# Smaller side steps behind gate tiles, and the last loads in another queue: an S4 convolution woven into a feed-forward network

## The chip, the core and the metric

The kernel runs on one core of a Trainium2 chip. The core has five engines with instruction streams of their own: PE (TensorE, matmuls), DVE (VectorE), ACT (ScalarE), POOL (GpSimd) and SP (SyncE, which here only issues DMAs). Each engine works its instructions off in order and waits on semaphores for what others produce. DMAs are issued by SP, ACT or POOL and carried by 16 DMA engines. The metric is the device time of one execution in microseconds (us). The kernel before takes 1129.19 us, the median of three runs (1126.59 to 1129.72).

## The reference

The input u has 2048 tokens of 576 features. Cut to what matters, the reference computes

```
xn  = layernorm(u)                                  # 2048 x 576
K   = Re( C * exp(dt*A*l) * dt*B  summed over 128 states ), l = 0..2047   # per feature
y   = irfft( rfft(pad(xn)) * rfft(pad(K)) )[:2048] + xn * Dskip            # long convolution
h   = silu(xn @ w1)                                 # w1: 576 x 4608
out = u + y + h @ w2                                # w2: 4608 x 576
```

All in 32-bit floats. The kernel gets that precision on PE by splitting an operand into a high and a low part and adding three products (high*high, high*low, low*high).

## The kernel before

**The main line: the feed-forward network.** Tokens come in four blocks of 512 and the 4608 hidden features in nine chunks of four tiles. A generator `ffn` runs over 36 blocks (half of the tokens, chunk, block in the half). For each it traces four `up` products (L291 to L293: `ph` <- split x times split `w1`, 14 matmuls of 512 columns, in one of two PSUM banks `ps1`) and four `down` products (L316: for each of two column halves, 12 matmuls `po`, in one of three banks `ps2`). ACT takes `ph` through Silu to `gf` (L299) and rounds it to `gh` (L300); DVE forms the low part `gl` (L301). DVE adds `po` to the accumulator `acc` (L320), which frees the bank. Weights are loaded by SP (`w1r` L247 to L249, one buffer; `w2r` L269, two buffers) and split by ACT (`w1h` L260, `w2h` L278) and DVE (`w1l` L262, `w2l` L280).

**The side line: the convolution.** A generator `side` yields at fractions of the main line's 288 steps, and `weave` advances it when the main line has come that far. Its stages, in order:

- `phase0`: token tiles 0 to 7 are loaded, normalised and transposed on PE for the first half.
- The *tables* (`natural`): from dt, A, B, C tables of the kernel K. Among their steps are four Tanh on ACT into `ex` (L447), a reciprocal root into `r` (L451, with a load of ACT's function table ahead of it, and one of Silu's behind), its Square (L452), DVE's products of `ex` and `r` (L457 to L459), and a store `dexp` by SP. In between, the *late tiles* 8, 10, 12 and 14 (two token tiles each) are loaded by SP into the single buffer `xj` (L164), normalised (statistics L180, DVE's half L189, ACT's half L194), transposed by DVE into `tr` (L226) and stored by eight DMAs of SP to `dxt` (L230) and one to `dxn`.
- `kgen` and `spread`: the kernel K and the tokens go through the first stage of a transform (`z` L646, `pu` L153 and L154); the results go to memory as `d1k` (staged by L659, then Dskip added by an accumulating DMA of POOL, L662) and `d1u` (L156).
- `spectral`: for each of 32 frequencies SP loads `ur` and `kr` from there (L746), ACT and DVE split them (`kh` L740, `kl` L741), PE transforms them (`pk`, `pu`, L754), DVE multiplies, PE transforms back (`pb`), and POOL stores the result `yo` to `d` (L705).
- `tail`: the last convolution step. For each of 16 token tiles `j` two DMAs load `ys` from `d` (`conv_load`, L761; eight buffers, six tiles ahead), eight matmuls give `py` (L774, two records each), and DVE adds it to the tile (L780). For tiles 0 to 7 the tile itself, with the feed-forward result, was put aside and is read back as `r0` (L716, four buffers), and POOL stores the output (L171).

**What sets the order.** The traced order is not the final one. A scheduler lays out each engine's instructions from its estimates of durations and from the dependences; `tc.high_priority()` favours some. `behind(ins)` pins what is traced in it to be issued after one named instruction, kept in the dictionary `pins` (the newest `gh`, `gl`, `sd` or weight load). Buffers add waits: a tile in a pool with n buffers waits until its nth predecessor is released. `gate_of(i)` gives the fraction at which the last `up` of block i is traced, so that a step placed there comes just behind that block's gate tiles `gf`, `gh`, `gl`.

Of the kernel before, what the change touches and what calls it, by code (L numbers as in the profile page):

```python
# [2 lines left out]

# [14 lines left out]
P = 128  # L18
# [4 lines left out]
NJ = 16  # L23
# [18 lines left out]
def kernel(  # L42
# [21 lines left out]
    nc = tc.nc  # L64
    FT = 4
# [68 lines left out]
    def behind(ins):  # L134
        return tc.issue_after(ins) if ins is not None else nullcontext()
# [24 lines left out]
    def load_x(j, pool, tag, engines):  # L160

        t = pool.tile([P, 2, D], F32, tag=tag, name=f"{tag}{j}")
        for ps, v, eng in quarters(xv, engines):
            eng.dma_start(t[ps], v[:, j:j + 2])  # L164
        pairs[j] = t
        return t[:, 0, :], t[:, 1, :]
# [30 lines left out]

    def phase0(p0, js):
        j0 = js[0]
        if j0 < 8:  # L200
            xs = load_x(j0, accp, "acc", (nc.sync, nc.scalar) if j0 < 4 else (nc.sync,))
            acc.update(zip(js, xs))
        else:
            xs = load_x(j0, p0, "xj", (nc.sync,))
        if j0:
            normed(p0, js, xs)
        else:
            for j, xj in zip(js, xs):
                normed(p0, (j,), (xj,))
# [23 lines left out]
    def ffn():  # L233
# [6 lines left out]
        def load_w1(half, c, t):  # L240

            f = c * FT + t
            first = half == 0 and c == 0
            r1 = (pa if first and t else wp).tile([P, 5, 2 * P], F32, tag="w1r", name="w1r", bufs=1)
            fs = slice(f * P, (f + 2) * P)
            eng = nc.gpsimd if first and t == 0 else nc.sync
            eng.dma_start(r1[:, 0:4, :], w1[0:512, fs].rearrange("(k p) f -> p k f", p=P))  # L247
            eng.dma_start(r1[0:64, 4, :], w1[512:576, fs])
            pins["load"] = eng.dma_start(r1[64:128, 4, :], w1[512:576, fs]).ins  # L249
            R1[half, c, t] = r1  # L250

        def split_w1(half, c, t):
# [12 lines left out]
        def load_w2(half, c, t):  # L265

            first = half == 0 and c == 0
            r2 = (pa if first and t > 1 else wp).tile([P, D], F32, tag="w2r", name="w2r", bufs=2)
            pins["load"] = nc.sync.dma_start(r2, w2v[:, c * FT + t, :]).ins  # L269
            R2[half, c, t] = r2  # L270

        def split_w2(half, c, t):
# [123 lines left out]
    def natural(nat):  # L396
# [5 lines left out]
        def tl(name):  # L402
            return nat.tile([NP, NT, NS], F32, tag=name, name=name)
# [49 lines left out]
        for i in range(0, 4 * D, D):  # L453
# [4 lines left out]
            v.scalar_tensor_tensor(r[:, c], e, 2.0, r[:, c], op0=ALU.add, op1=ALU.mult)  # L458
            v.scalar_tensor_tensor(ex[:, c], ex[:, c], 1.0, r[:, c], op0=ALU.add, op1=ALU.mult)  # L459
        nc.sync.dma_start(dexp, ex[:, :3 * D].rearrange("n (d k) -> n d k", k=3))  # L460
        pr, pi, t0, t1 = tl("pr"), tl("pi"), tl("t0"), tl("t1")
        v.tensor_mul(pr, cr, br)
        v.tensor_mul(t0, ci, bi)
# [199 lines left out]
                            dskip.unsqueeze(0).broadcast_to([32, D]), accum_op=ALU.add)  # L663

    def spectral():
        def front(k):
            if k % 2 == 0:
                mm = kl.tile([P, 2, 4, P], F32R, tag="mm", name="mm")
                nc.gpsimd.dma_start(mm, cm23[:, k:k + 2])
                mats.append(mm)  # L670
            mk = mats[-1][:, k % 2]
            us, ks = load_split(d1u[k * P:(k + 1) * P, :], "u"), load_split(d1k[k * P:(k + 1) * P, :], "k")
            ka = kl.tile([P, D], F32, tag="ka", name="ka")
            kb = kl.tile([P, D], F32, tag="kb", name="kb", bufs=1)
            y = kl.tile([P, D], F32, tag="y", name="y", bufs=1)
            y2 = kl.tile([P, D], F32, tag="y2", name="y2", bufs=1)
            for h in range(2):
                hs = slice(h * HD, (h + 1) * HD)
                pk = pss.tile([P, 512], F32, tag="pss", name="pk")
                mm3(pk[:, :HD], [(mk[:, 0], mk[:, 1], ks)], hs)  # L680
                nc.scalar.copy(ka[:64, hs], pk[:64, :HD])
                nc.scalar.copy(ka[64:, hs], pk[:64, :HD])
                nc.scalar.mul(kb[:64, hs], pk[64:, :HD], -1.0)
                nc.scalar.copy(kb[64:, hs], pk[64:, :HD])
                pu = pss.tile([P, 512], F32, tag="pss", name="pu2")
                mm3(pu[:, :HD], [(mk[:, 0], mk[:, 1], us)], hs)
                nc.vector.tensor_mul(y[:, hs], pu[:, :HD], ka[:, hs])
                nc.vector.tensor_mul(y2[:64, hs], pu[64:, :HD], kb[:64, hs])
                nc.vector.tensor_mul(y2[64:, hs], pu[:64, :HD], kb[64:, hs])
            nc.vector.tensor_add(y, y, y2)  # L690
            return mk, split_of(y, "y")

        mats = []
        nxt = front(0)
        for k in range(32):
            mk, ys = nxt
            if k < 31:
                nxt = front(k + 1)
            yo = kl.tile([P, D], F32, tag="yo", name="yo")
            for h in range(2):  # L700
                hs = slice(h * HD, (h + 1) * HD)
                pb = pss.tile([P, 512], F32, tag="pss", name="pb")
                mm3(pb[:, :HD], [(mk[:, 2], mk[:, 3], ys)], hs)
                nc.scalar.copy(yo[:, hs], pb[:, :HD])
            nc.gpsimd.dma_start(d2.rearrange("(p k) d -> k p d", k=32)[k], yo)  # L705
            yield 1 + (k + 1) / 32
# [3 lines left out]
    def tail():  # L710

        r0s = {}

        def load_r0(j):
            r0s[j] = yp.tile([P, 2, D], F32, tag="r0", name="r0", bufs=4)
            nc.sync.dma_start(r0s[j], dr0[j * P:(j + 2) * P, :].rearrange("(i p) d -> p i d", p=P))  # L716

        def last(j):
            conv_load(j + AHEAD, 8)
            add_conv(j, r0s[j - j % 2][:, j % 2, :])  # L720
            if j % 2:
                store(r0s[j - 1], j - 1, (nc.gpsimd,))

        steps, at = [], tail_at[0]
        for j in range(8):
            for f in (conv_load, load_r0)[:2 - j % 2]:
                steps.append((at, f, j))
                at += tail_at[1]
        steps += [(tail_at[2] + j * tail_at[3], last, j) for j in range(8)]
        for at, f, j in sorted(steps, key=lambda v: v[0]):  # L730
            yield at
            with behind(pins["load"]):
                f(j)

    yss = {}

    def split_of(t, tag):
        h = kl.tile([P, D], F32R, tag=tag + "h", name=tag + "h")
        l = kl.tile([P, D], F32R, tag=tag + "l", name=tag + "l")
        nc.scalar.copy(h, t)  # L740
        nc.vector.tensor_sub(l, t, h)  # L741
        return h, l

    def load_split(rows, tag):
        t = kl.tile([P, D], F32, tag=tag + "r", name=tag + "r")
        nc.sync.dma_start(t, rows)  # L746
        return split_of(t, tag)

    def mm3(dst, terms, hs):

# [6 lines left out]
    def conv_load(j, first=0):  # L757
        if first <= j < NJ:
            yss[j] = yp.tile([P, 4, HD], F32, tag="ys", name="ys", bufs=AHEAD + 2)
            for h in range(2):  # L760
                nc.sync.dma_start(yss[j][64 * h:64 * h + 64],  # L761
                                  d2[j * 256:(j + 1) * 256, h * HD:(h + 1) * HD].rearrange("(q r) d -> r q d", q=4))

    def add_conv(j, dst):
# [20 lines left out]

    def side():
        nonlocal s4, kl, yp, pa, tail_at
        marks = (0.13, 0.595, 0.822)
        tail_at = (0.895, 0.0045, 0.922, 0.005)
        with tc.tile_pool(name="pa", bufs=4) as pa:  # L790
            for js in ((0, 1), (2, 3), (4, 5), (6, 7)):
# [6 lines left out]
        with tc.tile_pool(name="kf", bufs=1) as kfp:  # L798
            for n in ("f", "phi"):
                kf[n] = kfp.tile([P, D], F32, name=n + "T")  # L800
            with tc.tile_pool(name="nat", bufs=1) as nat, tc.tile_pool(name="pb", bufs=1) as pb:
                nt = natural(nat)
                tiles = iter(range(8, NJ, 2))
                for at, tables in ((0.0, 1), (0.02, 0), (0.035, 0), (gate_of(1), 1), (0.06, 0), (gate_of(2), 1), (0.08, 0), (0.085, 1)):
                    yield at
                    if tables:
                        next(nt, None)
                    else:
                        j = next(tiles)
                        with behind(pins["gl"]):  # L810
                            phase0(pb, (j, j + 1))
            with behind(pins["sd"]):
                nc.gpsimd.dma_start(f1, cf1)
            nc.sync.dma_start(vt, cv)
            with tc.tile_pool(name="up", bufs=1) as up:
                sp = spread(up)
                for n, at in enumerate(kgen()):
                    if n > 1:
                        next(sp, None)
                    yield marks[0] + at * (marks[1] - marks[0])  # L820
                for _ in sp:
                    pass
# [98 lines left out]
```

## Time and profile before

| what | value |
|---|---|
| median of three runs | 1129.19 us (1126.59 to 1129.72) |
| the profiled execution | 1131.96 us, span 1130.2 us, granted clock 0.996 |
| PE busy | 1106.7 us, 98% of the span |
| DVE, ACT, POOL busy | 917.1, 708.7, 78.5 us |
| DMA | 148.56 MB, mean 131 GB/s |

The profile is of one execution. Its span is the time between the first and the last recorded instruction; 1.8 us of the execution's time lie outside it. A row of a group or of the timeline names a line, an engine, an operation and "out<-in" by tile names; the number before it is its duration. Square brackets give the idle time of the engine just before and what ended it ("3.67 <-DVE acc L320": 3.67 us, ended by DVE's instruction of line 320). In the table by windows each engine's busy time is followed by its count of instructions; the last three numbers are the clock granted to PE (1.00 is full), the mean busy share of the DMA engines, and GB/s. Consecutive instructions of one form are put together in a row ("x4"), and matmuls overlap, so a row's duration can be longer than the distance to the next.

### The profile page before, as it was taken

Reading aid. Unit: us, or ns where it says so; the run is one execution under the profiler, and the core shown is the slowest. Engines: PE = TensorE matmul, PEld = TensorE weight load, DVE = VectorE, ACT = ScalarE, POOL = GpSimd, SP = SyncE. Lnnn points to the kernel's source line nnn. Section 1 sums busy time; section 2 is a strip of 40 time slices with the busy share of each in tenths; the row PEclk is TensorE's granted clock in tenths of the full one; section 3 lists DMA queues with packets and bytes.
Section 4 is the critical chain, followed back from the end, with each engine's and each line's share of the span. In section 5 each row is a group of like instructions: output and inputs, shape, how many; then the busy total and the mean of one; then the engine's idle time right before and its main releaser. Section 6 shows DMA issues by size and latency. Waiting matters only on the chain.

```text
span 1130.2 us, 22881 instructions
## 1 busy us (share of the span) xinstructions
PE 1106.7 (98%) x9144; PEld 998.7 (88%) x9144; DVE 917.1 (81%) x1545; ACT 708.7 (63%) x1229; POOL 78.5 (7%) x130
## 2 busy tenths in 40 slices
PE   6999899999999999999999999999999999999998
PEld 5988799898888989999889998999999999998776
DVE  6698899999999999999999936887778778774433
ACT  4665356767677676676766727787777787772211
POOL 1110100000000000010000000000000000000110
PEclk9999899999999999999999999999999999999999
DMA  9346531334242625254743345554445455336971
GB/s 272 116 121 173 150 86 57 82 107 106 93 105 70 145 65 116 83 124 153 205 152 88 88 86 170 168 164 130 144 142 168 128 169 149 110 104 168 251 189 56
DMA packets 174971, 148.56 MB, mean 131 GB/s; under 512 B 110944, under 2 KB 141680, under 8 KB 174736
## 3 DMA queue, kind: packets, MB, share of 16 engines
q1 hardware_dynamic: 164768, 112.07, 37.6%
q0 software_dynamic: 9712, 34.14, 9.4%
q8 instruction: 72, 1.18, 0.4%
q10 hardware_dynamic: 384, 0.89, 0.3%
q14 instruction: 35, 0.29, 0.1%
HBM read 102.53 MB, written 44.61 MB: 130 GB/s over the span
## 4 chain that ended last, share of the span: by engine, by line
PE 86%; DVE 5%; DMA 5%; SPq 1%; issue 1%; ACT 0%; POOL 0%; DVEq 0%; POOLq 0%; ACTq 0%
PE po L316 36%; PE ph L291 30%; PE kp L631 3%; PE ph L292 3%; PE ph L293 2%; PE pk L754 2%; PE pu L754 2%; PE pb L754 2%; DMA w1r<-in_B_w_dram 2%; PE z L646 2%; PE pu L153 1%; DMA xj<-in_A_u_dram 1%; PE py L774 1%; PE pu L154 1%; DMA d1k<-stage 1%
## 5 line engine op out<-in xcount | busy, mean ns | idle before, releaser
L316 PE MATMUL po<-w2h,gh 128*128 128x288 f32 x1152 | 338.8, 297 | 6.4 <-DVE acc L320 5.7
L316 PE MATMUL po<-w2h,gl 128*128 128x288 f32 x1152 | 338.5, 297 | 1.0 <-DVE gl L301 1.0
L316 PE MATMUL po<-w2l,gh 128*128 128x288 f32 x1152 | 339.4, 296 | 0.0
L316 PEld LDWEIGHTS po<-w2h,gh 128*128 128x128 f32 x1152 | 216.1, 188 | 16.5 <-DVE acc L320 7.0
L316 PEld LDWEIGHTS po<-w2l,gh 128*128 128x128 f32 x1152 | 216.8, 188 | 4.3
L316 PEld LDWEIGHTS po<-w2h,gl 128*128 128x128 f32 x1152 | 216.5, 189 | 3.5 <-DVE gl L301 1.5
L299 ACT ACTIVATE gf<-ph 128x512 f32<-128x512 f32 (+1 forms) x148 | 86.5, 584 | 140.1 <-PE ph L293 124.7
L320 DVE TENSOR_TENSOR acc<-po,acc 128x288 f32<-128x288 f32 x288 | 126.3, 451 | 47.9 <-PE po L316 46.3
L291 PE MATMUL ph<-xh,w1h 128*128 128x512 f32 (+1 forms) x592 | 163.3, 391 | 0.5 <-ACT xh L123 0.5
L291 PE MATMUL ph<-xl,w1h 128*128 128x512 f32 (+1 forms) x592 | 161.5, 388 | 0.0
L291 PE MATMUL ph<-xh,w1l 128*128 128x512 f32 (+1 forms) x592 | 160.1, 386 | 0.0
L301 DVE TENSOR_TENSOR gl<-gf,gh 128x512 fp32r<-128x512 f32 (+1 forms) x148 | 98.7, 670 | 41.3 <-ACT gh L300 40.6
L291 PEld LDWEIGHTS ph<-xh,w1l 128*128 128x128 f32 x592 | 108.5, 189 | 20.1
L291 PEld LDWEIGHTS ph<-xl,w1h 128*128 128x128 f32 x592 | 108.5, 190 | 19.7
L291 PEld LDWEIGHTS ph<-xh,w1h 128*128 128x128 f32 x592 | 106.0, 191 | 20.0 <-issue 3.3
L300 ACT CAST gh<-gf 128x512 fp32r<-128x512 f32 (+1 forms) x148 | 89.5, 609 | 13.4 <-PE po L316 10.5
L278 ACT CAST w2h<-w2r 128x576 fp32r<-128x576 f32 x72 | 46.9, 672 | 30.6 <-PE po L316 19.5
L588 ACT ACTIVATE c<-th,magic 128x1040 f32<-128x1040 f32 x36 | 42.0, 1166 | 33.7 <-DVE C L611 25.7
L262 DVE TENSOR_TENSOR w1l<-w1r,w1h 128x640 fp32r<-128x640 f32 x72 | 56.9, 819 | 4.4 <-ACT w1h L260 4.3
L280 DVE TENSOR_TENSOR w2l<-w2r,w2h 128x576 fp32r<-128x576 f32 x72 | 53.4, 750 | 7.4 <-ACT w2h L278 7.2
L590 ACT ACTIVATE c<-th 128x1040 f32<-128x1040 f32 x36 | 38.7, 1076 | 32.6 <-DVE th L589 32.6
L292 PE MATMUL ph<-x,w1h 128*128 128x512 f32 (+1 forms) x148 | 57.2, 386 | 0.0
(182 smaller groups left out, 1836.9 us busy)
## 6 DMA issues: line engine op xcount, KB each, us to landing
w2r<-in_B_w_dram SPq DMA_DIRECT2D x72, 288.0 KB, 3.4
w1r<-in_B_w_dram SPq DMA_DIRECT2D x35, 512.0 KB, 3.9
d1u<-u POOLq DMA_DIRECT2D x32, 288.0 KB, 2.5
d1k<-stage SPq DMA_DIRECT2D x18, 512.0 KB, 7.7
ur<-d1u SPq DMA_DIRECT2D x32, 288.0 KB, 3.9
kr<-d1k SPq DMA_DIRECT2D x32, 288.0 KB, 2.8
d<-yo POOLq DMA_DIRECT2D x32, 288.0 KB, 3.9
ys<-d SPq DMA_DIRECT2D x32, 288.0 KB, 10.5
```

The source lines that it names most:

```text
L262: pins["w1l"] = nc.vector.tensor_sub(l1, src, h1).ins
L278: pins["w2h"] = nc.scalar.copy(h2, r2).ins
L280: nc.vector.tensor_sub(l2, r2, h2)
L291: nc.tensor.matmul(ph, w[:, kt, :], v[:, kt, a:e], start=n + kt == 0, stop=False)
L292: nc.tensor.matmul(ph, h1[:, 4, :], x4[:, a:e], start=False, stop=False)
L299: nc.scalar.activation(gf, ph, AF.Silu)
L300: pins["gh"] = nc.scalar.copy(gh, gf).ins
L301: pins["gl"] = nc.vector.tensor_sub(gl, gf, gh).ins
L316: pins["pe"] = nc.tensor.matmul(po[:, :HD], G[blk, t][g][:, js], W2[half, c, t][w][:, hs], start=n == 0, stop=n == 3 * FT - 1).ins
L320: nc.vector.tensor_add(acc[j][:, hs], po[:, :HD], acc[j][:, hs])
L588: nc.scalar.activation(c65, th, AF.Identity, bias=magic)
L754: nc.tensor.matmul(dst, st, mv[:, hs], start=n == 0, stop=n == 3 * len(terms) - 1)
```

## The change

Four things change, and nothing that is computed:

- Each late tile becomes two steps of a generator `late`: its load, and its normalisation, transposition and stores (pinned behind the newest `gl`). The tables get one more yield, behind the store `dexp`, and so come in five pieces. A new list places these eight and five steps at fractions between 0 and `gate_of(3)`, four of the tables' pieces at gates (0.017, 0.045, 0.073, 0.101); all but the first two are also pinned behind the newest `gl`.
- The side line's marks move by 0.006 to 0.01 of the main line: `kgen` starts at 0.14 instead of 0.13, `spectral` runs from 0.603 to 0.828 instead of 0.595 to 0.822.
- In `spectral` the loads of the first `ur` and `kr` become a step by themselves, their split another one (pinned behind the newest `gh`), and the first transforms a third.
- In `tail` the loads `ys` and `r0` are issued by POOL instead of SP, and the pin behind the newest weight load goes.

```diff
@@ -1,4 +1,5 @@
 import math
+from itertools import chain
 from contextlib import ExitStack, nullcontext
 
 import numpy as np
@@ -197,11 +198,8 @@
 
     def phase0(p0, js):
         j0 = js[0]
-        if j0 < 8:
-            xs = load_x(j0, accp, "acc", (nc.sync, nc.scalar) if j0 < 4 else (nc.sync,))
-            acc.update(zip(js, xs))
-        else:
-            xs = load_x(j0, p0, "xj", (nc.sync,))
+        xs = load_x(j0, accp, "acc", (nc.sync, nc.scalar) if j0 < 4 else (nc.sync,))
+        acc.update(zip(js, xs))
         if j0:
             normed(p0, js, xs)
         else:
@@ -246,7 +244,7 @@
             eng = nc.gpsimd if first and t == 0 else nc.sync
             eng.dma_start(r1[:, 0:4, :], w1[0:512, fs].rearrange("(k p) f -> p k f", p=P))
             eng.dma_start(r1[0:64, 4, :], w1[512:576, fs])
-            pins["load"] = eng.dma_start(r1[64:128, 4, :], w1[512:576, fs]).ins
+            eng.dma_start(r1[64:128, 4, :], w1[512:576, fs])
             R1[half, c, t] = r1
 
         def split_w1(half, c, t):
@@ -266,7 +264,7 @@
 
             first = half == 0 and c == 0
             r2 = (pa if first and t > 1 else wp).tile([P, D], F32, tag="w2r", name="w2r", bufs=2)
-            pins["load"] = nc.sync.dma_start(r2, w2v[:, c * FT + t, :]).ins
+            nc.sync.dma_start(r2, w2v[:, c * FT + t, :])
             R2[half, c, t] = r2
 
         def split_w2(half, c, t):
@@ -458,6 +456,7 @@
             v.scalar_tensor_tensor(r[:, c], e, 2.0, r[:, c], op0=ALU.add, op1=ALU.mult)
             v.scalar_tensor_tensor(ex[:, c], ex[:, c], 1.0, r[:, c], op0=ALU.add, op1=ALU.mult)
         nc.sync.dma_start(dexp, ex[:, :3 * D].rearrange("n (d k) -> n d k", k=3))
+        yield
         pr, pi, t0, t1 = tl("pr"), tl("pi"), tl("t0"), tl("t1")
         v.tensor_mul(pr, cr, br)
         v.tensor_mul(t0, ci, bi)
@@ -663,13 +662,17 @@
                             dskip.unsqueeze(0).broadcast_to([32, D]), accum_op=ALU.add)
 
     def spectral():
+        def operands(k):
+            rows = slice(k * P, (k + 1) * P)
+            return load_part(d1u[rows, :], "u"), load_part(d1k[rows, :], "k")
+
         def front(k):
             if k % 2 == 0:
                 mm = kl.tile([P, 2, 4, P], F32R, tag="mm", name="mm")
                 nc.gpsimd.dma_start(mm, cm23[:, k:k + 2])
                 mats.append(mm)
             mk = mats[-1][:, k % 2]
-            us, ks = load_split(d1u[k * P:(k + 1) * P, :], "u"), load_split(d1k[k * P:(k + 1) * P, :], "k")
+            us, ks = ops.pop(k) if k in ops else (split_of(t, n) for t, n in zip(operands(k), "uk"))
             ka = kl.tile([P, D], F32, tag="ka", name="ka")
             kb = kl.tile([P, D], F32, tag="kb", name="kb", bufs=1)
             y = kl.tile([P, D], F32, tag="y", name="y", bufs=1)
@@ -691,6 +694,11 @@
             return mk, split_of(y, "y")
 
         mats = []
+        first = operands(0)
+        yield 1.1
+        with behind(pins["gh"]):
+            ops = {0: [split_of(t, n) for t, n in zip(first, "uk")]}
+        yield 1.12
         nxt = front(0)
         for k in range(32):
             mk, ys = nxt
@@ -713,7 +721,7 @@
 
         def load_r0(j):
             r0s[j] = yp.tile([P, 2, D], F32, tag="r0", name="r0", bufs=4)
-            nc.sync.dma_start(r0s[j], dr0[j * P:(j + 2) * P, :].rearrange("(i p) d -> p i d", p=P))
+            nc.gpsimd.dma_start(r0s[j], dr0[j * P:(j + 2) * P, :].rearrange("(i p) d -> p i d", p=P))
 
         def last(j):
             conv_load(j + AHEAD, 8)
@@ -729,8 +737,7 @@
         steps += [(tail_at[2] + j * tail_at[3], last, j) for j in range(8)]
         for at, f, j in sorted(steps, key=lambda v: v[0]):
             yield at
-            with behind(pins["load"]):
-                f(j)
+            f(j)
 
     yss = {}
 
@@ -741,10 +748,10 @@
         nc.vector.tensor_sub(l, t, h)
         return h, l
 
-    def load_split(rows, tag):
+    def load_part(rows, tag):
         t = kl.tile([P, D], F32, tag=tag + "r", name=tag + "r")
         nc.sync.dma_start(t, rows)
-        return split_of(t, tag)
+        return t
 
     def mm3(dst, terms, hs):
 
@@ -758,7 +765,7 @@
         if first <= j < NJ:
             yss[j] = yp.tile([P, 4, HD], F32, tag="ys", name="ys", bufs=AHEAD + 2)
             for h in range(2):
-                nc.sync.dma_start(yss[j][64 * h:64 * h + 64],
+                nc.gpsimd.dma_start(yss[j][64 * h:64 * h + 64],
                                   d2[j * 256:(j + 1) * 256, h * HD:(h + 1) * HD].rearrange("(q r) d -> r q d", q=4))
 
     def add_conv(j, dst):
@@ -785,7 +792,7 @@
 
     def side():
         nonlocal s4, kl, yp, pa, tail_at
-        marks = (0.13, 0.595, 0.822)
+        marks = (0.14, 0.603, 0.828)
         tail_at = (0.895, 0.0045, 0.922, 0.005)
         with tc.tile_pool(name="pa", bufs=4) as pa:
             for js in ((0, 1), (2, 3), (4, 5), (6, 7)):
@@ -800,15 +807,19 @@
                 kf[n] = kfp.tile([P, D], F32, name=n + "T")
             with tc.tile_pool(name="nat", bufs=1) as nat, tc.tile_pool(name="pb", bufs=1) as pb:
                 nt = natural(nat)
-                tiles = iter(range(8, NJ, 2))
-                for at, tables in ((0.0, 1), (0.02, 0), (0.035, 0), (gate_of(1), 1), (0.06, 0), (gate_of(2), 1), (0.08, 0), (0.085, 1)):
+                def late(j):
+
+                    xs = load_x(j, pb, "xj", (nc.sync,))
+                    yield
+                    with behind(pins["gl"]):
+                        normed(pb, (j, j + 1), xs)
+                    yield
+
+                tiles = chain.from_iterable(late(j) for j in range(8, NJ, 2))
+                for at, todo in ((0.0, nt), (0.0, tiles), (gate_of(0), nt), (0.024, tiles), (0.026, tiles), (0.035, tiles), (0.037, tiles), (gate_of(1), nt), (0.055, tiles), (0.06, tiles), (gate_of(2), nt), (0.085, tiles), (gate_of(3), nt)):
                     yield at
-                    if tables:
-                        next(nt, None)
-                    else:
-                        j = next(tiles)
-                        with behind(pins["gl"]):
-                            phase0(pb, (j, j + 1))
+                    with behind(pins["gl"] if at else None):
+                        next(todo, None)
             with behind(pins["sd"]):
                 nc.gpsimd.dma_start(f1, cf1)
             nc.sync.dma_start(vt, cv)
```

The instructions of each engine stay the same in number and shape, apart from 36 DMA issues that go from SP to POOL; the scheduler's order changes on all engines.

## The prediction

> **What bounds the kernel now.** First the page's busy times and the chain that ended last:
>
> ```profile
> PE 1106.7 (98%) x9144; PEld 998.7 (88%) x9144; DVE 917.1 (81%) x1545; ACT 708.7 (63%) x1229; POOL 78.5 (7%) x130
> PE 86%; DVE 5%; DMA 5%; SPq 1%; issue 1%; ACT 0%; POOL 0%; DVEq 0%; POOLq 0%; ACTq 0%
> ```
>
> PE is busy for 1106.7 of 1130.2 us and 86% of the chain, and the change takes no matmul away. It can only win or lose PE's idle time and slow clock, so the next view is PE's waits:
>
> ```profile
> PE pt L122 <- DVE xn L189: 9.0, 1, 9.0
> PE po L316 <- DVE acc L320: 5.7, 2, 3.7
> PE pk L754 <- ACT kh L740: 1.3, 1, 1.3
> PE po L316 <- DVE gl L301: 1.0, 2, 0.7
> PE po L316 <- ACT w2h L278: 0.7, 1, 0.7
> ```
>
> The first 9.0 us are the start of the kernel, whose order the change leaves. Then the table by 20 us (busy us of PE, PEld, DVE, ACT, POOL; granted clock; DMA share), which places the rest:
>
> ```profile
> 100.00:120.00 20.00, 20.00 (x123) 18.08 (x121) 19.68 (x34) 5.85 (x9) 1.74 (x1) 1.00 0.57 142
> 120.00:140.00 20.00, 15.66 (x87) 14.58 (x86) 16.39 (x32) 6.20 (x10) 4.63 (x3) 0.83 0.43 147
> 680.00:700.00 20.00, 18.65 (x105) 16.27 (x104) 12.55 (x22) 13.07 (x28) 0.00 (x0) 1.00 0.63 197
> 1040.00:1060.00 20.00, 18.02 (x133) 13.48 (x132) 8.81 (x17) 5.85 (x10) 1.97 (x4) 1.00 0.94 236
> ```
>
> Three places, and the 0.7 us at 97. Only that after 120 also loses clock (0.83), after DVE was busy for 19.68 of 20 us. Last the timelines, where square brackets hold the idle time before an instruction and its releaser:
>
> ```profile
> 120.78 1.54 DVE L180 BATCH_NORM_STATS2 st<-xj 128x6 f32<-128x288 f32 x4 [1.10 <-DMA xj<-in_A_u_dram]
> 123.81 0.40 PE L316 MATMUL po<-w2h,gh 128*128 128x288 f32 x1 [3.67 <-DVE acc L320]
> 125.81 0.61 PE L316 MATMUL po<-w2h,gl 128*128 128x288 f32 x1 [0.67 <-DVE gl L301]
> 687.37 0.40 PE L754 MATMUL pk<-kh,mm 128*128 128x288 f32 x1 [1.35 <-ACT kh L740]
> 1055.51 1.35 ACT L260 CAST w1h<-w1r 128x640 fp32r<-128x640 f32 x2 [4.40 <-DMA w1r<-in_B_w_dram]
> 1058.25 0.40 PE L316 MATMUL po<-w2h,gh 128*128 128x288 f32 x1 [1.98 <-DVE acc L320]
> ```
>
> **The change part by part.** *Counts.* Every engine keeps its instructions. 36 DMA issues (32 ys, four r0) go from SP to POOL; everything else is another order on the same engines. At 0.58 us an issue on SP (the median of ys) SP is relieved of 21 us; at 0.54 us (POOL's d<-yo) POOL takes up 19 us, beside 78.5 busy of 1130. Neither is time of PE by itself.
>
> *The stall after 120, removed.* DVE's statistics of late tile 14 wait 1.10 us for xj, whose four loads SP issues at 115.87 to 117.31 behind four of the previous tile's dxt stores (0.51 us each); behind it stand 1.54 of statistics, 1.15 of a wt product, then the acc addition that frees PE's bank. PE loses 3.67 + 0.67. Then 19 po matmuls take 4.55 us (126.22 to 130.77) where such matmuls before and behind start every 0.135 us, 2.0 us too much; eight ph take 2.37 instead of 1.84, 0.5 too much; the po at 125.81 holds PE for 0.41, 0.3 too much. Clock: 2.8. With the 0.74 at 97 (w2h, whose load stood between xj loads in SP's queue) the early losses are 7.9 us. The new order spreads the tiles, each load apart from its normalisation, and the tables in five pieces. I laid the rows' durations along the new order: DVE then reaches every acc of 95 to 135 ahead of PE, by 3 us at the least (in before it falls to 0.1 at the last ones ahead of the stall). Bounds for what stays there: 0, and 1.7 if tile 12's xj lands as late as tile 14's (the 1.10 and a 0.6 cast behind it). I take 0.8.
>
> *A new stall, 57 to 79 us.* In before the reciprocal root r stands here:
>
> ```profile
> 51.12 3.13 ACT L447 ACTIVATE ex<-lrT 128x576 f32<-128x576 f32 x4
> 54.15 0.58 ACT L299 ACTIVATE gf<-ph 128x512 f32<-128x512 f32 x1
> 66.02 1.28 ACT L451 ACT_TABLE_LOAD   x1
> 67.31 2.22 ACT L451 ACTIVATE r<-ex,neg 128x2304 f32<-128x2304 f32 x1
> 71.25 2.13 ACT L452 ACTIVATE r<-r 128x2304 f32<-128x2304 f32 x1
> 73.40 1.28 ACT L299 ACT_TABLE_LOAD   x1
> ```
>
> In the new order its table load, r and the reload for Silu come directly behind the four Tanh and ahead of that gf: 54.2 + 1.28 + 2.22 + 1.28 + 0.58 = 59.6 instead of 54.7. Queued behind gf stand ACT's late tile, the Square of 2.13 and gh. PE has ph and nine po until about 57.9, then needs the bank that gf frees: 1.7 us. The next po waits for gh behind the Square: 0.85; the next ph behind two w1h casts: 0.65; on DVE an acc that follows statistics of xj and the table products comes 0.75 late. Sum 4.0; bounds 2.5 (the last two covered) and 6 (each hole half longer). Each hole is under the 1.98 us which, at 1058, cost no clock, so I add none. Early part: 7.9 off, 4.0 + 0.8 on: **-3.1**.
>
> The Trainium skill, "TensorE: Matmul & The Clock Gate", Part 1, says that the array falls to half clock after an idle window of about 3.4 us and returns after one as long of work. The 3.67 us that lost clock and the 1.35 and 1.98 us that lost none agree; by the rule the holes above lose none either, which is the same sum.
>
> *The middle, 140 to 660: 0.* No PE stall there now; DVE is busy for about 16 of 20 us and covers the moved steps. Without that cover one hole of the size of those seen, 1 to 2 us.
>
> *Spectral's first operands: -1.35.* Now the chain runs z 662.8, stage copies, d1k<-stage 8.51 us, Dskip's accumulation 3.87, kr 6.47, kh 686.64: 24.5 us. In the new order 33.7 us of PE's work lie between the last z and the first pk, so 9 us of cover take the wait's place. On SP the kr load waits for the accumulation with w2r loads behind it, as before. Bounds: -1.35, and 0 if those w2r come late next.
>
> *The last step's loads.* Spectral now ends nearer to the end: summed by rows, 1011.3 us of PE's work stand ahead of its last pb, 1002.4 before, so the y inverse transforms (py) have about 9 us less to spread over. Supply: in before the last d store is issued at 1025.88 and ys begin 2.6 us behind it. If that holds, the first pair comes about 5.6 us behind the last pb; each pair or r0 is 590 KB, 2.4 us at 250 GB/s (between the 236 and 276 GB/s of 1040 to 1080). So the pairs are there at about 10, 15, 17, 19, 24, 27 us; the py need them at 13, 18, 19, 23, 30, 35. By the landings seen (median 10.5, most 12.8 us), the fourth pair, issued some 10 us behind the last pb, comes at 20.5 to 22.8, just in time: 0. Other bound: 9 us, all of the compression. I take 0, the nearer, since issue times, rate and landings are all rows of this operation. POOL's out stores (0.49 us each) stand ahead of later ys and wait for r of DVE; before the eleventh pair nothing needed stands behind one.
>
> *w1r at 1041: -2.0.* It was issued 0.02 us after DVE freed its buffer, so it was not late; it took 11.82 us to land among SP's ys (w1r's median is 3.9):
>
> ```profile
> 1043.59 11.82 DMA w1r<-in_B_w_dram
> 1056.27 1.56 DVE w1l L262 x2
> ```
>
> PE would need it 2 us earlier. In the new order the ys are in another queue and SP holds weights alone. Bounds: 0 (no faster beside the same bytes) and -2.0. I take -2.0: 8 us of landing are over the median and 2 suffice.
>
> The Trainium skill, "DMA: Bandwidth & Descriptors", says under "Issuing engines are not separate DMA queues" that transfers from any engine run and interleave on the same 16 DMA engines, and another issuer saves only issue time. By that rule alone w1r would still take about 11.8 us and the term would be 0; its section "Queues, rings and completion order" has each engine take queues in turn, which speaks for the -2.0. No run here shows which.
>
> **Sum.** -3.1 - 1.35 + 0 - 2.0 = -6.4. On the profiled execution (1131.96 us, span 1130.2 and 1.8 around it) that gives 1125.5; this execution is 2.8 us above the median of the three runs, so from 1129.2 I predict 1122.8 us. Its own range, by the bounds: 1118 to 1126.
>
> **The rivals.** *All is gained.* The ACT block is covered, since PE's order can give it more po than my walk. All 7.9 + 1.35 + 2.0 = 11.3 go: 1118. Against it: ph uses two banks, and both wait for ACT.
>
> *The stall only moves.* If gf comes 1.9 us later than worked out (its late tile's xj or the reload late), the first hole grows from 1.7 to 3.67 and, as at 123.81, the clock halves: 4.8 + 1.9 + 2.8 = 9.5 instead of 7.9, +1.6; with -1.35 and -2.0 about 1127.4. For it: DVE is busy for 18.64 of 20 us in 60 to 80. Against: PE's clock is full there now.
>
> *Slower: the last loads.* DMA share is 0.94 to 1.05 from 1040 to 1080; if the late start passes to the end whole, PE waits up to 9 us in py, and w1r (2.0) stays late: 1129.2 - 3.1 - 1.35 + 9 = 1133.8, 1136.6 with one loss of clock. It decides for slower from a wait of 8 us. For it: the share. Against: in before ys go on until 1081 because buffers free slowly, so the later ones have slack.
>
> *It does nothing.* Excluded as to the order, as the instructions do move; as to time it is the case at 1127.
>
> **How the numbers follow.** Within 0.3% (3.4 us: 1125.8 to 1132.6) is what a measurement here can't tell from no change. Forecast 0.48 and all gained 0.08, both faster; of the forecast's own 0.48, 0.02 reach over 1125.8. The stall moves, or two smaller terms fail, 0.24: same. Slower 0.20, by the last loads (0.12) or a DVE queue that comes late in the early part with loss of clock (0.08). So faster 0.54, same 0.26, slower 0.20. The range from 1117 to 1134 leaves out a little below and half of the slower cases above.
>
> **What would show it.** Right: no idle time over 0.5 us before po and clock 1.00 from 95 to 140; some 4 us of PE idle between 57 and 79, released by ACT gf and gh; pk at the start of spectral without a wait; w1r near 1045 landing in under 10 us; py without waits for ys. Wrong: clock under 1.00 between 55 and 80 (the stall moves), po waiting for acc later than 80, PE waiting for ys, or a wait of w2h or kh at the start of spectral.

## The result and the profile after

The changed kernel takes 1135.94 us (median of five runs, 1133.63 to 1138.39) against 1129.3 us before: ratio 1.0061, 95% interval 1.0038 to 1.0083. The forecast was 1122.8 us, a gain, with a range up to 1134; the change makes the kernel slower. The profiled execution took 1137.08 us, its span is 1135.3 us.

The page's busy times and chain after:

```profile
PE 1109.7 (98%) x9144; PEld 998.9 (88%) x9144; DVE 916.3 (81%) x1545; ACT 710.3 (63%) x1229; POOL 94.1 (8%) x166
PE 72%; DVE 8%; issue 8%; DMA 7%; ACT 3%; SPq 1%; POOL 1%; ACTq 0%; DVEq 0%; POOLq 0%
```

PE is still the bound; the chain now goes through POOL's issues and the `ys` ("issue" 8%). PE's waits after:

```profile
PE py L781 <- DMA ys<-d: 2.5, 2, 2.2
PE py L781 <- DVE r L787: 2.4, 1, 2.4
PE ph L289 <- ACT gf L297: 2.1, 3, 1.7
PE po L314 <- ACT w2h L276: 1.4, 2, 1.0
PE po L314 <- DVE acc L318: 1.2, 1, 1.2
PE po L314 <- DVE gl L299: 1.2, 2, 0.8
```

The 5.7 us for acc and the 1.3 for kh are gone. In their place stand waits for gf and acc (early), for w2h and gl (from 537 to 636 us), and for `py` in the tail. The table by windows after (the columns are those shown of before):

```profile
60.00:80.00 20.00, 18.27 (x94) 15.05 (x93) 16.14 (x29) 10.46 (x16) 1.00 (x1) 1.00 0.42 107
...
120.00:140.00 20.00, 20.00 (x128) 18.38 (x127) 19.97 (x37) 10.07 (x15) 1.43 (x2) 1.00 0.32 91
...
680.00:700.00 20.00, 20.00 (x113) 17.75 (x112) 8.66 (x14) 10.20 (x18) 0.00 (x0) 1.00 0.60 187
...
1040.00:1060.00 20.00, 17.04 (x123) 12.27 (x121) 4.03 (x8) 3.97 (x7) 9.54 (x16) 0.91 1.05 250
1060.00:1080.00 20.00, 18.31 (x142) 14.97 (x142) 10.75 (x22) 4.48 (x8) 7.52 (x14) 0.91 1.04 257
```

The stall and the low clock of 120 to 140 (0.83 before) have left that place; in the tail the clock is 0.91 for 40 us, a loss of 0.09 x 40 = 3.6 us beside the waits.

To put a number on each place I gave every matmul of PE its usual distance to the next start (ph 0.227 us, po 0.133 and so on), summed these, and compared the times at which two executions have done the same sum. Both have the same matmuls, so where the orders agree again the difference is the time won or lost so far. After against before:

| stretch | forecast | measured | read at |
|---|---|---|---|
| 57 to 79: ACT's block | +4.0 | +4.6 | -0.6 at 55 us, +4.0 at 95 us |
| early part, all | -3.1 | -3.85 | 150 us |
| middle | 0 | +4.7 | +0.8 at 650 us |
| spectral's start | -1.35 | -1.65 | -0.8 at 700 us and still at 860 us |
| tail | -2.0 | +6.3 | +5.49 at PE's last instruction |

Two terms failed, the middle and the tail (the last step's loads and w1r together). Each gives back more than the early part wins.

### The profile page after: what moved, and what is told of

Read it like the earlier page. It is cut to its first block, busy times and chain, and to the rows that moved or that the text cites. A ratio compares the mean times of both kernels' runs of the same rounds, so it can differ in the third digit from the quotient of the medians.

```text
span 1135.3 us, 22868 instructions
## 1 busy us (share of the span) xinstructions
PE 1109.7 (98%) x9144; PEld 998.9 (88%) x9144; DVE 916.3 (81%) x1545; ACT 710.3 (63%) x1229; POOL 94.1 (8%) x166
## 3 DMA queue, kind: packets, MB, share of 16 engines
q8 instruction: 72, 1.18, 0.5%
## 4 chain that ended last, share of the span: by engine, by line
PE 72%; DVE 8%; issue 8%; DMA 7%; ACT 3%; SPq 1%; POOL 1%; ACTq 0%; DVEq 0%; POOLq 0%
PE po L314 31%; PE ph L289 25%; DMA ys<-d 4%; PE kp L630 3%; PE ph L291 2%; PE ph L290 2%; PE pk L761 2%; PE pu L761 2%; PE pb L761 2%; PE z L645 1%; DMA d1k<-stage 1%; DMA xj<-in_A_u_dram 1%; PE pu L154 1%; DMA w2r<-in_B_w_dram 1%; DVE acc L318 1%
```

## The experiments

Medians are of three rounds; "before" ran beside each group, at 1128.84, 1129.49, 1129.76 and 1129.64 us.

### One part at a time: tail and marks

Undoing the tail's part of the changed kernel (pin included):

```diff
-            nc.gpsimd.dma_start(r0s[j], ...
+            nc.sync.dma_start(r0s[j], ...
-                nc.gpsimd.dma_start(yss[j][64 * h:64 * h + 64],
+                nc.sync.dma_start(yss[j][64 * h:64 * h + 64],
-            f(j)
+            with behind(pins["load"]):
+                f(j)
```

> The changed kernel with the tail's part undone: ys and r0 again issued by SP, pinned behind the newest weight load; early order, spectral's first operands and the later marks stay. From the two traces, the place where the changed kernel loses most is the tail (PE waits 2.24 for ys and 2.40 behind w1l, clock 0.91 in 1040 to 1080, some 6.3 us more than before). Queue theory (POOL's queue beside SP's makes w1r late): the tail costs what it did before, 2.0 us, w1r lands in some 12 us instead of 17.5, and the time is 1135.9 - 6.3 = about 1129.6. Timing theory (spectral ends 9 us later, so the loads of ys begin at 1037.7 instead of 1028.5, whatever the queue): PE still waits for ys or w1l in the tail and the time stays at 1133 to 1137.

Measured: 1137.92 us (ratio 1.0078, 1.0055 to 1.0101): not better. Only the marks put back:

```diff
-        marks = (0.14, 0.603, 0.828)
+        marks = (0.13, 0.595, 0.822)
```

> The changed kernel with the old marks (0.13, 0.595, 0.822); the early order, spectral's first operands and POOL's tail loads stay. Timing theory: the ys begin near 1029 again, the tail's waits go, 1135.9 - 6.3 = about 1129.6. Queue theory: w1r still takes over 15 us, the tail still costs about 6 us. On the middle (537 to 636 us, where the changed kernel loses about 4.7 us of PE's time that the kernel before does not lose): if the marks cause it, another 4.7 us go (timing and marks: 1125; queue and marks: 1131); if the early order causes it by putting DVE behind, it stays (1130 or 1136).

Measured: 1137.24 us (1.0070, 1.0047 to 1.0093): not better either; spectral ends early here (last d store at 1021.0 us), and PE waits 10.01 us for acc at 1061. Both edits together:

> The early order and spectral's first operands alone; tail and marks as in the kernel before. If these two bring what the traces show for them (3.85 us at 57 to 140 us, 1.65 at the start of spectral) and the middle's loss belongs to the marks: 1129.3 - 3.85 - 1.65 = about 1123.8. If the middle's loss belongs to the early order: 1128.5.

Measured: 1128.35 us (0.9998, 0.9983 to 1.0012): the loss is gone, but nothing is won. And the tail's part alone, in the kernel before (the first diff the other way round):

> The kernel before with only the tail's part of the change: ys and r0 issued by POOL, without the pin. Queue theory: w1r in the tail lands late (15 us or more instead of 11.8), PE's wait behind w1l grows and the time is up to 1129.3 + 6.3 = 1135.6. Timing theory: spectral ends as before, so ys are in time and the tail costs 0 to 2 us: 1127 to 1130.

Measured: 1138.13 us (1.0082, 1.0055 to 1.0109). So POOL's loads alone cost 9 us, and in the changed order the marks with SP's loads cost as much (1137.92 against 1128.35); the two are not additive. The timelines show one way to both: the last w1r comes late, DVE's w1l behind it holds up acc. Rows of three timelines, in this order the kernel before with POOL's loads, the changed kernel, and the changed one with SP's loads:

```profile
1062.48 1.35 ACT L260 CAST w1h<-w1r 128x640 fp32r<-128x640 f32 x2 [12.40 <-DMA w1r<-in_B_w_dram]
...
1065.22 0.61 PE L316 MATMUL po<-w2h,gh 128*128 128x288 f32 x1 [9.98 <-DVE acc L320]
```

```profile
1052.54 1.18 PE L781 MATMUL py<-ys,s 64*32 64x288 f32 x8 [2.24 <-DMA ys<-d]
...
1059.68 1.35 ACT L258 CAST w1h<-w1r 128x640 fp32r<-128x640 f32 x2 [9.55 <-DMA w1r<-in_B_w_dram]
...
1061.69 0.69 PE L781 MATMUL py<-ys,s 64*32 64x288 f32 x8 [2.40 <-DVE r L787]
```

```profile
1046.94 0.38 SPq L245 DMA_DIRECT2D w1r<-in_B_w_dram  x1
1048.19 1.27 SPq L246 DMA_DIRECT2D w1r<-in_B_w_dram  x1
1050.27 0.49 SPq L247 DMA_DIRECT2D w1r<-in_B_w_dram  x1
...
1065.69 0.61 PE L314 MATMUL po<-w2h,gh 128*128 128x288 f32 x1 [5.82 <-DVE acc L318]
```

With POOL's loads w1r is issued in time (1040.4) and its first two pieces take 18.3 and 19.3 us to land (the first of the three timelines; 15.9 to 18.1 us in the changed kernel). With SP's loads and the late end of spectral it lands in 11.8 to 14.5 us, but is issued only at 1046.9 to 1050.3: in SP's queue it stands behind loads of ys and r0, and by the chain of waits its last piece goes out when an r0 issued at 1040.2 has landed, 10.0 us later. The kernel before had neither: w1r issued at 1041.4 to 1043.6, landing after 11.8 to 13.3 us. Counted from issues and landings, neither SP nor POOL has more than eight of its transfers in flight in the tail of any of the traces: with eight out, the next often goes 0.02 us (SP) or 0.28 us (POOL) after one has landed. What sets this limit no run shows.

The marks alone, in the kernel before:

> The kernel before with the later marks (0.14, 0.603, 0.828) alone; ys and r0 on SP with their pin. The kernel with the later marks and SP's tail lost some 8 us in the tail against the kernel before. Timing theory (a later end of spectral by itself makes the last loads collide with w1r): about 1128.8 + 8 = 1137, with PE waiting some 5 us behind w1l and for ys in the tail. If instead the missing early stall or spectral's first operands are needed for the collision, it stays near 1129 to 1131. For the middle (140 to 640 us): if the marks alone make DVE come late there, 1 to 2 us of PE's idle time; if it is the early order, none.

Measured: 1131.61 us (1.0025, 1.0009 to 1.0041). The expected 8 us are not in the median, and the last store of d is issued at 1025.7 us as before, and not at 1032 to 1034 us as in the changed kernels: in these runs the later marks move spectral's end only together with the first operands' own steps. But the ten runs spread from 1129.5 to 1137.1 us, and the profiled execution, the slowest, loses 5.0 us of progress in the tail all the same: a ys issued at 1065.4 takes 14.8 us to land, PE waits 2.16 us for it at 1080.3, and the matmuls behind run at half clock until 1086. Why ys are so late there stays open. In the middle this execution loses 1.9 us (idle 0.79 at 520 and 0.77 at 634 us).

### What w1r and the late end cost by themselves

ys and r0 on POOL in the kernel before, and the last w1r loaded at the start of the tail into a buffer of its own:

```diff
+        yield tail_at[0]
+        r1 = yp.tile([P, 5, 2 * P], F32, tag="w1x", name="w1x", bufs=1)
+        ... (its three loads by nc.sync; load_w1 then skips this tile)
```

> The kernel before with ys and r0 on POOL, and the last w1r loaded at the start of the tail into a buffer of its own, ahead of the burst of ys. If w1r's late landing is the whole cause of POOL's cost, PE's wait behind w1l goes and with it the 2.0 us of before: 1126 to 1128. If late ys or POOL's queue itself cost time too, PE waits for ys (py) instead and the time stays above 1132.

Measured: 1126.65 us (0.9975, 0.9962 to 0.9987). Both the 10 us at 1065 and the 2.0 of before are gone; 1.08 us of waiting for ys stay, at 1074 us, with half clock behind them until 1080 (2.7 us of progress in all). w1r's late landing is thus nearly the whole cost of POOL's loads, as long as spectral ends as before. The same buffer in the changed kernel:

> The changed kernel, all four parts, with the last w1r loaded at the start of the tail into a buffer of its own. If w1r's late landing is the cause of the changed kernel's slowness, its 6.3 us in the tail go and the 2.0 of before too: 1135.9 - 6.3 - 2.0 = 1127.6, at most 1129.6. If the late end of spectral costs by itself (ys late for py): PE still waits for ys, 1131 to 1134.

Measured: 1136.78 us (1.0079, 1.0062 to 1.0095): no help. Its chain of waits in the tail:

```profile
1032.59 2.40 DMA d<-yo
...
1036.05 1.26 POOL ys L779 x2
1037.31 0.72 POOL r L728
1038.03 0.62 POOL ys L779
1038.64 11.63 DMA ys<-d
...
1050.32 1.19 PE py L792 x8
```

Here PE waits for ys itself (2.94 us at 1050.32), and that buffer's own load, issued at 1035.3, is in the same crowd (0.83 us at 1045). The last store of d is issued at 1032.6; ys begin 3.5 us behind. Is it the end of spectral or its start? The third mark alone put back in that kernel:

```diff
-        marks = (0.14, 0.603, 0.828)
+        marks = (0.14, 0.603, 0.822)
```

> The changed kernel with the last w1r in a buffer of its own (1136.8 us so far) and only the third mark put back, 0.822 instead of 0.828, so that spectral ends as early as before. If the late end of spectral (last d store at 1032 to 1034 us instead of 1021 to 1026) is the cause of the tail's loss: ys begin near 1026, py doesn't wait for them, and the time falls by some 8 us to 1128 to 1130, the middle's loss of 4 to 5 us staying. If the later start (0.603) does it: 1135 to 1137.

Measured: 1130.96 us (1.0006, 0.9991 to 1.0022), last d store at 1026.6 us. 5.8 of the 7 us go with the end alone. The two profiled executions differ by 4.8 us in the tail (8.1 us lost against 3.3) and by 1.1 in the middle. Waits of 0.48 and 1.85 us for ys stay, and the clock does not hold behind the second: four ph take 1.91 us there, 1.09 at full clock.

```profile
1075.30 0.69 PE L792 MATMUL py<-ys,s 64*32 64x288 f32 x8 [1.85 <-DMA ys<-d]
...
1078.82 1.91 PE L293 MATMUL ph<-xl,w1h 128*128 128x512 f32 x4
```

Now the other way round. The base is a fast version: the kernel before with POOL's loads, the own w1r and spectral's first operands.

> The early order of before, spectral's first operands, old marks, ys and r0 on POOL, the last w1r in a buffer of its own: the kernel at 1126.65 us plus spectral's part. If the wait of 0.8 to 1.35 us at the first pk goes and nothing takes its place: 1125.3. If spectral's part by itself puts DVE's last steps of kgen late: 1127.

In it the third mark alone is put late:

```diff
-        marks = (0.13, 0.595, 0.822)
+        marks = (0.13, 0.595, 0.828)
```

> The kernel at 1126.4 us (early order of before, spectral's first operands, ys and r0 on POOL, own w1r) with the third mark alone put late, 0.828 instead of 0.822. If the late end of spectral is the cause: the last d store some 7 us later, py waits for ys by 3 to 5 us and the clock falls, 1131 to 1135. If it takes the later start too, 1126 to 1128.

Measured: without it 1126.42 us (0.9977, 0.9963 to 0.9990), last d store at 1021.8; with it 1129.13 us (1.0003, 0.9983 to 1.0024), last d store at 1025.3 and a wait for ys of 1.46 us in the profiled execution. This is the fastest of its ten runs; the others spread from 1127.3 to 1136.5 us, so the late end costs 2.7 us in the median, less than the 5 to 9 expected, and its size changes from run to run; what decides it in one execution no trace shows. The first pk does not wait in the fast version, but it does not wait in the kernel at 1126.65 us either, which has spectral as before; the two times, 0.2 us apart, show no gain from spectral's steps.

Why does w1r take 18 us beside POOL's loads? What the DMA queues moved from 1040 to 1055 us, before and in the kernel before with POOL's loads (q1 is SP's, q0 POOL's; packets, MB, share of the 16 engines):

```profile
q1 hardware_dynamic: 2875, 3.56, 96.6%
q0 software_dynamic: 192, 0.59, 10.0%
```

```profile
q0 software_dynamic: 864, 3.30, 90.1%
q1 hardware_dynamic: 444, 0.45, 14.1%
```

On POOL's queue a packet is 3.8 KB, on SP's w1r's are 1 KB; for two packets of POOL's one of SP's went, and w1r got an eighth of the bytes. To make POOL's packets small I parted the four pieces of a ys partition by padding:

```diff
-            yss[j] = yp.tile([P, 4, HD], F32, tag="ys", ...
+            yss[j] = yp.tile([P, 4, HD + 8], F32, tag="ys", ...
```

> The kernel before with ys and r0 on POOL (1138.1 us as measured), and eight unused columns behind each 288 of the ys tile, so that the four pieces of a partition no longer lie side by side. In the trace POOL's queue moves packets of 3.8 KB beside w1r's of 1 KB in SP's queue, 864 against 444 packets from 1040 to 1055. Packet theory (the queues take turns by packet, so w1r gets bytes in the ratio of packet sizes): with ys packets of 1.15 KB, w1r gets about half of the rate, lands in some 8 us instead of 18 and the time is 1129 to 1132. If the share is not set by packets, or the padding does not part them, 1138.

Measured: 1137.82 us (1.0065, 1.0050 to 1.0080), but POOL's packets are still 2.96 MB / 787 = 3.8 KB: the padding did not part them. The run tells nothing on the share, and what sets it stays open. The Trainium skill, "DMA: Bandwidth & Descriptors", section "Queues, rings and completion order", has the engines take queues in turn by packets; the packets' sizes here fit a small share of bytes for w1r, but not the one-to-two count of packets.

### The early part and the middle

The early order with the root r at the gate of block 1 (tail and marks of before):

```diff
-... (0.0, tiles), (gate_of(0), nt), (0.024, tiles), ... (gate_of(1), nt), (0.055, tiles), (0.06, tiles), (gate_of(2), nt), ...
+... (0.0, tiles), (0.024, tiles), ... (gate_of(1), nt), (0.055, tiles), (0.06, tiles), (0.065, nt), (gate_of(2), nt), ...
```

> Early order and spectral's first operands as changed, tail and marks as before, and the tables' second piece (the root r with its two table loads on ACT) moved from the gate of block 0 to that of block 1, the next piece to 0.065. If r's place on ACT causes the waits at 59 to 79 us (1.65, 0.30 and 0.41 us shown as idle, some 3 us of PE's progress), these go and the time falls from 1128.3 to about 1125.5. Rival: DVE is the limit there and PE waits elsewhere for the same time: 1128.

Measured: 1128.43 us (0.9985, 0.9975 to 0.9996). The waits at 59 to 79 us are gone, so r's place on ACT made them; but 0.98 and 1.73 us of idle time come at 122 and 125 us, and progress at 150 us is 5.5 us ahead of the kernel before, as much as without the move (5.4). The rival was right on the time; but ACT (gh and w1h), not DVE, ends these two waits.

The early part of the change alone, put into the kernel before:

> The kernel before with the early part of the change alone (late tiles and tables in smaller steps); spectral's first operands, marks and tail as before. The three kernels that hold the early order lose some 3 us of PE's progress between 150 and 640 us, those with the order of before lose none (1.5 with the later marks). If the early order does this by putting DVE's later steps in another order: idle time of PE at 515 to 575 again, progress at 650 us only 2 to 3 us ahead of the kernel before, time 1127 to 1129.5. If it is spectral's first operands (their traced steps let the scheduler order the last of kgen otherwise), the middle loses nothing and the time is 1125 to 1127.

Measured: 1126.97 us (0.9981, 0.9967 to 0.9995). The time lies where the two ranges meet; the progress decides. It is 5.2 us ahead at 160 us, 1.0 at 650 and 1.7 at 720, with nearly the wait at the first pk that the kernel before has (1.18 us for 1.35): the early order by itself loses 3.5 to 4.3 us in the middle, of which 1.7 are shown as idle time and the rest lies in shorter delays. This kernel is nevertheless 2.8 us faster than before. Of the 4.6 us by which this execution leads at its end, the trace has 3.0 in the tail: the last store of d is issued at 1008.4 us, w1r lands after 7.4 to 7.8 us, and PE does not wait behind w1l. PE's waits in this kernel:

```profile
PE po L314 <- DVE gl L299: 1.5, 3, 0.6
PE po L314 <- DVE w2l L278: 1.4, 3, 0.9
PE pk L757 <- ACT kh L743: 1.2, 1, 1.2
```

DVE's timeline at one of them, with no idle time in any row, shows gl standing behind five steps of kgen (its gh was ready at 538.3 us):

```profile
537.86 1.22 DVE L598 TENSOR_TENSOR C<-pw 128x1024 f32<-128x1024 f32 x1
539.00 1.24 DVE L588 SCALAR_TENSOR_TENSOR th<-c,th 128x1040 f32<-128x1040 f32 x1
540.15 0.76 DVE L594 TENSOR_TENSOR C<-pw,wb 128x256 f32<-128x256 f32 x2
540.82 1.22 DVE L598 TENSOR_TENSOR C<-pw 128x1024 f32<-128x1024 f32 x1
541.96 0.69 DVE L299 TENSOR_TENSOR gl<-gf,gh 128x512 fp32r<-128x512 f32 x1
```

PE's next po starts behind this gl at 542.7, after 0.64 us of idle time. None of the profiled executions with the early order of before and its marks (five beside the first) loses anything there.

Late tile 14 alone moved ahead of the tables' third piece, in the fast version (the order of before):

```diff
-... (0.06, 0), (gate_of(2), 1), (0.08, 0), (0.085, 1)
+... (0.06, 0), (0.07, 0), (gate_of(2), 1), (0.085, 1)
```

> The same kernel at 1126.4 us with late tile 14 at 0.070 of the main line instead of 0.080, ahead of the tables' third piece. If the stall at 123 us comes from that tile's late load and the work it puts ahead of acc on DVE, the idle 3.2 us there shrink and the clock holds: 1122 to 1124. If DVE is behind there whatever the order: 1126.

Measured: 1126.22 us (0.9974, 0.9962 to 0.9985), no different from 1126.42, with 3.26 us idle at 123.3 as before. But the two traces hold the same instructions in the same order on all five engines: the edit did not change the schedule, and the run tells nothing on the tile's place. The early order as a whole removes this stall; which of its moves does so stays open.

### All that helps, together

Early order with r later, spectral's first operands, old marks, POOL's loads, own w1r:

> Early order with r at the gate of block 1, spectral's first operands, old marks, ys and r0 on POOL, and the last w1r in a buffer of its own. If the gains add up: 1128.4 (the same with SP's tail) less 2 = about 1126; if all that the profiles show is lasting, 1124.

Measured: 1126.17 us (0.9981, 0.9965 to 0.9996). The gains do not add up: the early order's part is lost again, with idle times of 0.80, 0.59 and 0.28 us between 515 and 575 us. The versions at 1126.2 to 1126.7 us are a quarter per cent under the kernel before, and POOL's loads with the last w1r in its own buffer are enough for it; the early part alone comes to nearly the same (1126.97).

## Why the prediction was wrong

- **The stall after 120 (removed, 7.9 us with the one at 97): right in place, too large in size.** It is gone (clock 1.00, no idle time over 0.5 us from 95 to 140). But its cost in the kernel before is not the same in each execution: in seven others with the early order of before, progress at 150 us stood 0.4, 0.5, 1.9, 2.6, 2.8, 2.8 and 3.1 us ahead of the one that I had read, where the slowest had 20 matmuls at half clock and others 10 to 13. The eight with the early order besides the changed kernel stand 5.2 to 6.4 ahead. With the two executions first read, the medians are 2.3 and 5.4: a gain of 3.1 that met the forecast partly by luck, as the execution read before was a slow one there and the one after gained least.
- **ACT's block, +4.0: right.** The order came as read (table load, r, reload, gf at 58.44), and so did the first hole (1.65 us for 1.7); the holes together cost 4.6. The clock held.
- **DVE from 95 to 135, +0.8: 0 measured.**
- **The middle, 0: wrong.** The step said that DVE, busy for about 16 of 20 us, covers the moved steps. That is the share of one window (16.18 us from 140 to 160); from 140 to 660 us DVE was busy for 490 of 520 us in the kernel before, 18.8 of 20, so there was little cover. From 200 to 300 us it is busy for 99.5 of 100 us in the changed kernel (97.9 before). At 542 us the trace shows a gl late because large steps stand ahead of it in DVE's queue; that the other waits come about in the same way is argued, not shown. By 650 us the early order costs 3.7 to 4.3 us in the five executions that hold it with the old marks, the marks alone 1.9 in one. The sentence's own fallback, "1 to 2 us without that cover", was for one hole, and there were four.
- **Spectral's first operands, -1.35: right in the trace, not shown in the median.** It was -1.65 in the changed kernel. But the wait that it removes changes from execution to execution: with the order, spectral and marks of before it is 1.35 us in the one first read, 0.79 in another, and absent in two (with POOL's loads and padded ys, and with POOL's loads and the own w1r).
- **The last step's loads, 0: wrong, the main failure.** The supply was set against py's demand to within a microsecond or two. Counted from the last pb, the third pair was worked out for 17 us and its py for 19; it landed at 19.2, and PE was ready for it at 17.1, so PE waited 2.24 us. Behind it ys took up to 13.6 us, and POOL waited 13 times for an earlier ys to land before it issued the next (10.0 us together). The rival "slower: the last loads" (0.12) is what happened, with the mechanism that it named: spectral's late end passed on to py, and w1r stayed late. Its price of 1133.8 to 1136.6 us held by luck: it had up to 9 us of waiting in py, where 2.5 are measured, and nothing for a w1r that lands later than before or for the 4.7 us of the middle.
- **w1r, -2.0: wrong in sign.** In a queue of its own w1r took 15.9 to 18.1 us instead of 11.8 to 13.3. The sentence cited from "DMA: Bandwidth & Descriptors" in the Trainium skill, that the issuing engine gives a transfer no DMA engines of its own, was nearer than my term, but w1r took longer than by that rule too. SP's queue, a line in which later ys stand behind w1r, had presumably protected it; how the queues share the engines no run shows.
- **The clock.** I added none for holes under 1.98 us, and that held in the early part. But I priced no loss of clock for the tail: the 2.24 and the 2.40 us each brought po at 0.24 us instead of 0.13 behind them (1054.05 to 1055.7 and 1063.3 to 1066.2). The rule of the Trainium skill that I had found in agreement ("TensorE: Matmul & The Clock Gate", Part 1, an idle window of about 3.4 us) would have let these pass, and so the 1.08 and 1.85 us behind which other runs lost clock; here the measurement decides.
- **The sum's own range, 1118 to 1126: wrong.** The bounds named for its terms add up to 1120.4 and 1129.0 without the 9 us of the last loads, and to 1138.0 with them. The bound that came nearest to happening was left out.

## What to carry to other kernels

A time at which transfers must be in is no term of 0 when supply and demand meet within a microsecond or two: take the longest landing seen, ask which other load shares the burst, and price that one too. To move loads to another queue takes away the order among them, and this order may have been what let one urgent load through; give the urgent load its own buffer ahead of the burst first. Where an in-order engine is busy nearly all the time (here DVE, 490 of 520 us), a reordering can bring waits hundreds of microseconds behind the place that was changed; read its share over the whole stretch and not in one window. After an edit to traced positions, compare the order in the trace before reading the time: the schedule may not have changed at all.

## What was not expected of the hardware

- The length of an idle time did not decide whether half clock followed. In the tail it followed 1.08, 1.85, 2.16, 2.24, 2.40 and 2.94 us right before small py matmuls; it did not follow 0.93, 0.99 and 1.46 us before such ones, nor 1.98, 1.74 and 1.56 us before po, nor 1.65 us at 59.
- The same stall of 3.2 to 3.7 us at 123 us cost 20 matmuls at half clock in some executions and 10 to 13 in others.
- Beside POOL's queue with packets of 3.8 KB, 640 KB on SP's queue with packets of 1 KB took 16 to 21 us; where all stood in SP's one queue, 11 to 14.5 (7.4 to 7.8 where spectral had ended 17 us earlier).
- Neither SP nor POOL had more than eight transfers in flight in the tail of any of the 17 traces.
